# One shared ring of five PSUM buffers for scores and maxima, and the router's first batch, three gathers, tile 0's first half-product and the weight re-packing moved to other steps

## The chip, the cores and the metric

The kernel runs on 1 core of one Trainium2 chip. The metric is the device time of one execution in microseconds (us), of which the kernel before has three timed runs and one profiled execution.

## The reference

Three stages follow one another on the same 1536 tokens of 512 numbers.

```python
# 1. attention within hash buckets: 2 batches, 8 heads, 768 rows of 64
mask = q_bucket[:, :, :, None] == k_bucket[:, :, None, :]
scores = np.where(mask, q @ k.T / 8, -1e9)
attn = exp(scores - scores.max(-1)); attn /= attn.sum(-1) + 1e-9
x = attn @ v                                  # -> 1536 x 512
# 2. mixture of experts: 8 experts, each token goes to one
logits = x @ w_gate + modality_bias[modality_id]
e_idx = argmax(logits); gate = softmax(logits)[e_idx]
out[tokens of e] = gate * (relu(x @ w1[e]) @ w2[e])     # 512 -> 1024 -> 512
# 3. dense layer
h = out @ w_in                                # 512 -> 2048
out = (max(h, 0) + alpha * min(h, 0)) @ w_out
```

## The kernel before, in words

Everything is written for one core with the order of each engine's work fixed by hand: the program is emitted step by step, and each engine runs its part in that order. Wherever full precision is wanted, an fp32 operand is split in a rounded half ("hi", usually a copy on ScalarE) and a remainder ("lo", a subtraction), and a product becomes three matmuls.

**Attention** is a loop of 102 steps. Step s handles key block s % 6 (128 keys) of head s // 6 (16 heads, so scores end with step 95). In each step:
- `ST(s,0)` and `ST(s,1)` make the scores of one block against two halves of 384 queries (two matmuls each, lines 807 and 808) in a PSUM buffer "st" from the pool `pst` of 2, and ScalarE's exp reads them (line 809).
- `MAX(u,0)` and `MAX(u,1)` make, up to 11 steps ahead of the scores, the product from which the row maxima are taken (line 775) in a buffer "mxp" from the pool `psm` of 3; VectorE reduces it (line 776). From step 7 there is one unit u in a step; the last is in step 85. The order on TensorE is ST(s,0), MAX(u,0), ST(s,1), MAX(u,1).
- `EL(s-1)` splits the exponentials E: Eh by ScalarE (line 812), El by GpSimd, and from block 88 (`ELD`) by VectorE (line 813).
- `AV(s)` multiplies them by v four steps later, for two blocks in every second step (lines 821 to 823). It has one buffer, which `NORM(h)` (lines 834 to 836) frees at the end of a head. After heads 7 and 15, NORM sends the 768 finished tokens to DRAM (`x_d`, line 838).
- Small work takes turns in a pool `misc` of 2 PSUM buffers: the split of v (701 to 706), its sums (712 to 715), the signs of the hash (748 to 755), the rows of maxima (781 to 788, with a small DMA), transposes `T` of finished tokens (172, copied at 175) and the logits `L` (186 to 192).

**The hook** runs at the end of each step s and carries what is ahead of its stage. `rr.first` is the router of batch 0 as a generator of eleven pieces, one at each step of `PLAN["first"]`: softmax and one-hots (`S`), counts by matmul (`R`), the most frequent expert ("star", `star` and `star2`), ranks (`adjust`), `GATE`, and the row numbers of three tiles of 128 tokens (`pre`). It works in a `misc` buffer, on VectorE, line 203 to 275. At step 71 the buffer BIG[0] of batch 0's tokens becomes its scratch. From step 89 on, when the router is ready, three indirect DMAs `GA` on GpSimd fetch the three tiles' tokens (line 596). `W1` at the steps of `PLAN["w1"]` splits the star expert's first weights in eight pieces of 128x512: hi by GpSimd, lo by VectorE (lines 571 and 572). At step 96 tile 0's tokens are transposed and split (556 to 558).

**Experts.** After the attention, tile t of 128 tokens needs `G1(t,0)` and `G1(t,1)` (12 matmuls each, line 1007, then relu), `TH` (8 transposes, hi/lo, lines 1018 to 1021), `G2` (24 matmuls, line 1030) and `Y`. `TX(t+1)` (986 to 993) prepares the next tile's tokens. Tiles 0 to 2 are the star's; their order around `G1(0, 0)` is written out by hand, with `W2` splitting the second weights as they land (line 569 with 128x1024). Tiles 3 to 12 are the loop `for t in range(NPRE, NBASE)`; new weights are loaded and split only where the expert of a tile differs from the last one's (`changed`): first weights by `load(t + 1, which=(1,))` and `W1s`, second by `load(t, which=(2,))` and `W2`.

**Dense weights.** In six of these tiles (`PRE`) a piece of the third stage's weights comes in beside: `CL(p)` loads 1 MB through SyncE's queue, and `CV(p, 0..4)` re-packs it, once on ScalarE (line 1134) and four times on VectorE (1136 to 1142). All share the landing place x2, so that a CL waits for the CV before it. In a tile t, CL stands at the beginning, ahead of `load(t, which=(2,))`, and CV at the end. In tile 12 (`last`), `CL(LP[0])` also goes to x2.

The third stage is 16 x 3 rounds of 24 matmuls (lines 1300 and 1326).

## Time and profile before

| | |
|---|---|
| three timed runs | 720.5, 715.89, 720.5 us (median 720.5) |
| profiled execution | 719.58 us, of which the span from the first to the last instruction is 717.5 us |
| TensorE busy | 684.8 us, 95% of the span |
| mean granted clock of TensorE | 0.967 of full speed |

A time in the trace is in us from the span's start. A matmul's shown end is modelled, and starts are closer together than the shown lengths, so a busy TensorE need not be one at its peak: what it loses is in its idle time, and in stretches with a granted clock of half speed. The clock has two levels, 0.5 and 1.0 of full speed; a window's figure is a mean over both.

### The profile page before, as it was taken

How to read it: one execution, taken by the hardware profiler on the slowest of the kernel's cores; microseconds unless marked ns; L12 is line 12 of the kernel's file. 1: busy time of each engine (PE TensorE's matmuls, PEld its weight loads, DVE VectorE, ACT ScalarE, POOL GpSimd, SP SyncE). 2: the span in 40 equal slices, each digit the busy share in tenths (PEclk: the TensorE clock that was granted, in tenths of full speed). 3: DMA queues.
4: the chain of work that ended last, by engine and by line, in shares of the span. 5: the costliest groups of instructions: out<-in, count | busy, mean ns of one | idle time of the engine just before them, and what ended most of it. 6: DMA issues, size and time to landing. Idle time of an engine off the chain costs nothing. (4 is left out here: it accounts for less than half of the span.)

```text
span 717.5 us, 13119 instructions
## 1 busy us (share of the span) xinstructions
PE 684.8 (95%) x5032; PEld 564.2 (79%) x5032; DVE 443.1 (62%) x902; ACT 329.5 (46%) x555; POOL 239.3 (33%) x212
## 2 busy tenths in 40 slices
PE   6889999999998889999989999999999999999996
PEld 4668888898887778778878877788888888888884
DVE  6768788787789677516444547999644344433432
ACT  5457887887866735225334337666411111211111
POOL 8367998887975800210100011012011010010002
PEclk8569999999999999999999999999999999999999
DMA  8257854865624123226522265434001000010001
GB/s 208 62 158 176 178 150 91 178 180 127 134 98 163 47 90 131 69 69 221 206 88 89 83 226 175 132 118 147 0 23 67 0 30 1 0 59 0 1 1 58
DMA packets 31229, 72.40 MB, mean 101 GB/s; under 512 B 6924, under 2 KB 7014, under 8 KB 30902
## 3 DMA queue, kind: packets, MB, share of 16 engines
q1 hardware_dynamic: 28068, 61.78, 30.3%
q0 software_dynamic: 2960, 9.70, 4.1%
q8 instruction: 41, 0.67, 0.4%
q14 instruction: 30, 0.25, 0.1%
q10 hardware_dynamic: 130, 0.00, 0.0%
HBM read 79.15 MB, written 12.06 MB: 127 GB/s over the span
## 5 line engine op out<-in xcount | busy, mean ns | idle before, releaser
L813 POOL TENSOR_TENSOR El<-E,Eh 128x768 f16<-128x768 f32 x88 | 144.3, 1652 | 48.6 <-ACT Eh L812 17.4
L809 ACT ACTIVATE E<-st 128x384 f32<-128x384 f32 x192 | 89.4, 491 | 67.3 <-PE st L808 65.3
L776 DVE TENSOR_REDUCE mx<-mxp 128x1 f32<-128x384 f32 x189 | 96.9, 548 | 12.8 <-PE mxp L775 12.3
L569 ACT ACTIVATE gh<-gf 128x512 fp32r<-128x512 f32 x48 | 30.3, 630 | 143.9 <-PE o L1326 133.4
L812 ACT ACTIVATE Eh<-E 128x768 f16<-128x768 f32 x96 | 81.0, 845 | 0.0
L807 PE MATMUL st<-op 97*128 97x384 f32 x192 | 76.8, 400 | 3.5 <-DMA op<-mr 2.4
L775 PE MATMUL mxp<-op 76*128 76x384 f32 x189 | 68.0, 370 | 4.8 <-DVE mx L776 3.1
L572 DVE TENSOR_TENSOR gl<-gf,gh 128x512 fp32r<-128x512 f32 x48 | 33.1, 690 | 59.7 <-ACT gh L569 57.7
L1030 PE MATMUL y<-op,hh 128*128 128x512 f32 x208 | 69.6, 402 | 0.0
L1300 PE MATMUL h<-big,op 128*128 128x512 f32 x256 | 68.6, 395 | 0.0
L1343 POOL DMA_INDIRECT out_dram<-x,did x12 | 11.8, 984 | 169.1 <-DVE x L1340 89.8
L808 PE MATMUL st<-op 128*128 128x384 f32 x192 | 68.0, 354 | 0.0
L1007 PE MATMUL g<-op,xh 128*128 128x512 f32 x192 | 63.6, 403 | 1.2 <-DVEq L1087 1.0
L1326 PE MATMUL o<-op,gh 128*128 128x512 f32 x192 | 64.2, 395 | 0.0
L821 PE MATMUL av<-vh,Eh 128*128 128x65 f16 x576 | 60.0, 198 | 1.5 <-DVE big L836 1.5
L821 PEld LDWEIGHTS <-Eh 128*128 128x128 f16 x576 | 53.5, 100 | 8.9 <-issue 6.6
L822 PE MATMUL av<-vl,Eh 128*128 128x64 f16 x576 | 59.5, 196 | 0.0
L823 PE MATMUL av<-vh,El 128*128 128x65 f16 x576 | 59.2, 196 | 0.0
L1300 PEld LDWEIGHTS h<-big,op 128*128 128x128 f32 x256 | 47.9, 187 | 11.8
L822 PEld LDWEIGHTS <-Eh 128*128 128x128 f16 x576 | 54.1, 101 | 0.1
L823 PEld LDWEIGHTS <-El 128*128 128x128 f16 x576 | 54.0, 100 | 0.0
L1184 POOL DMA_INDIRECT yg<-ys,dpos x10 | 11.7, 1168 | 122.5 <-DMA ys<-ysb 67.7
(401 smaller groups left out, 1519.8 us busy)
## 6 DMA issues: line engine op xcount, KB each, us to landing
r<-in_moe_w_dram SPq DMA_DIRECT2D x42, 1024.0 KB
op<-B SPq DMA_DIRECT2D x32, 192.0 KB
op<-in_moe_w_in_dram SPq DMA_DIRECT2D x6, 1024.0 KB
op<-A SPq DMA_DIRECT2D x28, 192.0 KB
op<-A SPq DMA_DIRECT2D x13, 384.0 KB
op<-in_moe_w_out_dram SPq DMA_DIRECT2D x4, 1024.0 KB
ys<-ysb SPq DMA_DIRECT2D x13, 256.0 KB
big<-in_q_dram SPq DMA_DIRECT2D x17, 192.0 KB
```

Of the source, the lines that this page charges most:

```text
L775: mm(p[:,0:384],t[0:76,2,c*128:(c+1)*128],t[0:76,1,a*384:a*384+384],start=True,stop=True)
L776: nc.vector.tensor_reduce(out=mx[h][:,c,a:a+1],in_=p[:,0:384],axis=AX.X,op=ALU.max)
L807: mm(p[:,0:384],t[0:97,1,js],t[0:97,2,qs],start=True,stop=False)
L808: mm(p[:,0:384],t[:,0,js],t[:,3,qs],start=False,stop=True)
L809: nc.scalar.activation(E[s][0][:,qs],p[:,0:384],AF.Exp,scale=0.125)
L812: nc.scalar.activation(eh,e,AF.Copy)
L813: (nc.vector if s>=ELD else nc.gpsimd).tensor_tensor(out=el,in0=e,in1=eh,op=ALU.subtract)
L821: mm(a[:,c*65:c*65+65],eh[:,cs],VH[h//4%2][:,j,h%4,:],start=(j==0 and c==0),stop=False,skip_group_check=True)
L822: mm(a[:,c*65:c*65+64],eh[:,cs],VL[h//4%2][:,j,h%4,:],start=False,stop=False,skip_group_check=True)
L823: mm(a[:,c*65:c*65+65],el[:,cs],VH[h//4%2][:,j,h%4,:],start=False,stop=False,skip_group_check=True)
L1030: nc.tensor.matmul(yps[t], a[:, ks], b[:, kk], start=(kk == 0 and n == 0), stop=(kk == 7 and n == 2))
L1300: nc.tensor.matmul(p, terms[t][0][:, kk, cs], terms[t][1][:, kk], start=(n == 0), stop=(n == 11))
```

## The change

1. The pools `pst` (2) and `psm` (3) become one pool `ps5` of 5 buffers, which ST and MAX take in turn in their order on TensorE.
2. The router's first batch runs at steps 57 to 73, not 72 to 87. Its scratch BIG[0] is taken over at step 56; the zeros for `ys` (filled by GpSimd) lie elsewhere in it. `star2` takes a buffer of its own, with one more small copy (`k8`).
3. The three gathers are issued at steps 78, 81 and 84.
4. For n = 6 (tokens of batch 1), the transposes are at steps 88 and 89, not 89 and 90, and the logits' halves at 94 and 92, not 95 and 91.
5. W1's hi goes from GpSimd to ScalarE, and its last four pieces are at steps 96 to 99. Of blocks 91 and 94, Eh goes from ScalarE to VectorE.
6. `G1(0, 0)` runs within the attention: 6 matmuls at step 98, before the last pair of AV, and 6 and the relu at step 100, behind it.
7. CL moves behind the next tile's `TX` and `W1s`, and so behind `load(t, which=(2,))` on SyncE; the CV of a piece runs one tile later, ahead of the next CL. In tile 12, the CV of piece 6 stands behind `Y(11)` and ahead of `CL(LP[0])`.

```diff
-    ... w1=(91, 92, 93, 94, 95, 96, 98, 99), ..., first=(72, 74, 75, 76, 78, 80, 81, 82, 84, 86, 87),
+    ... w1=(91, 92, 93, 94, 96, 97, 98, 99), ga=(78, 81, 84), ..., x6=(0, 1, 6, 4), first=(57, 58, 59, 60, 62, 63, 64, 67, 71, 72, 73),
...
-    pst = pool(psA, "pst", PS[0], space=PSUM)
-    psm = pool(psA, "psm", PS[1], space=PSUM)
+    ps5 = pool(psA, "ps5", 5, space=PSUM)
...
+        if s == 56:
+            BIG[0] = big(0)
+            rr.late(rtmp, BIG[0])
+            R["z"] = BIG[0][:, 784:1296]
+            nc.gpsimd.memset(R["z"], 0.0)
+            R["first"] = rr.first(misc)
...
-        if s >= 89 and rr.ready and "pre" not in R:
-            R["pre"] = s
-            for t in range(NPRE):
-                GA(t)
+        if s in PLAN["ga"]:
+            GA(PLAN["ga"].index(s))
...
+        if s in (98, 100):
+            h, lo = R["x0"]
+            w1h, w1l = R["w1"]
+            if s == 98:
+                R["g0"] = GP()
+            p = R["g0"]
+            for kk in range(s - 98, s - 96):
+                ks = slice(kk * 128, kk * 128 + 128)
+                for n, (a, b) in enumerate(((h, w1h), (lo, w1h), (h, w1l))):
+                    nc.tensor.matmul(p, a[:, ks], b[:, kk, 0:512], start=(kk == 0 and n == 0), stop=(kk == 3 and n == 2))
+            if s == 100:
+                R["hr0"] = BIG[0][:, 1536:2048]
+                nc.scalar.activation(R["hr0"], p, AF.Relu)
...
-            W1(i // 4, i % 4, i % 4 + 1, nc.vector, nc.gpsimd)
+            W1(i // 4, i % 4, i % 4 + 1)
...
-        p=psm.tile([128,512],F32,tag="mxp",name="mxp") if pool is None else pst.tile([128,512],F32,tag="st",name="stm")
+        p=ps5.tile([128,512],F32,tag="s",name="mxp")
...
-        p=pst.tile([128,512],F32,tag="st",name="st")
+        p=ps5.tile([128,512],F32,tag="s",name="st")
...
-        nc.scalar.activation(eh,e,AF.Copy)
+        if s in (91,94): nc.vector.tensor_copy(eh,e)
+        else: nc.scalar.activation(eh,e,AF.Copy)
...
-    G1(0, 0)
+    hr[0] = R["hr0"], mp.tile([128, 1024], F32, tag="hr", name="hr", bufs=2)[:, 0:512]
...
-        if t in PRE:
-            CL(PRE[t])
         if t == last:
             G2(t - 1)
             Y(t - 1)
+            for i in range(5):
+                CV(PRE[t - 1], i)
             CL(LP[0])
         load(t, *er[t], which=(2,))
...
+        if t - 1 in PRE and t < last:
+            for i in range(5):
+                CV(PRE[t - 1], i)
+        if t in PRE and t < last:
+            CL(PRE[t])
...
-        if t in PRE:
-            for i in range(5):
-                CV(PRE[t], i)
```

## Rows read from the trace of the kernel before

**Rows 1.** The page: busy time of the engines, and the granted clock in 40 slices.

```profile
PE 684.8 (95%) x5032; PEld 564.2 (79%) x5032; DVE 443.1 (62%) x902; ACT 329.5 (46%) x555; POOL 239.3 (33%) x212
...
PEclk8569999999999999999999999999999999999999
```

**Rows 2.** Windows of steps 57-64, 65-72, 73-85, 86-101: length, PE, PEld, DVE, ACT, POOL, clock.

```profile
164.10:181.98 17.88, 17.04 (x240) 14.85 (x238) 14.08 (x41) 13.32 (x26) 13.71 (x9) 1.00 0.44 93
181.98:199.41 17.43, 17.11 (x230) 14.75 (x230) 13.48 (x32) 14.59 (x28) 15.86 (x11) 1.00 0.63 138
199.41:233.65 34.24, 31.00 (x441) 27.21 (x441) 30.24 (x109) 22.96 (x44) 22.17 (x15) 1.00 0.40 136
233.65:262.55 28.90, 24.63 (x376) 20.95 (x372) 22.68 (x42) 17.63 (x33) 15.56 (x16) 0.88 0.11 30
```

**Rows 3.** Windows of VectorE, sums: the router's first five bursts, then its last three.

```profile
sum 9.20, DVE 7.89; mean DVE 1.58
...
sum 2.97, DVE 2.56; mean DVE 0.85
```

**Rows 4.** Waits of TensorE: line waited at, releaser, us in total, times, longest.

```profile
PE mxp L775 <- DVE mx L776: 3.1, 6, 1.4
...
PE av L821 <- DVE big L836: 1.5, 1, 1.5
...
PE misc L172 <- DVE big L175: 1.3, 2, 1.0
```

**Rows 5.** Timeline of VectorE, steps 91 to 93: start, us, line, tiles.

```profile
246.19 4.47 DVE L813 TENSOR_TENSOR El<-E,Eh 128x768 f16<-128x768 f32 x1
...
251.59 0.95 DVE L813 TENSOR_TENSOR El<-E,Eh 128x768 f16<-128x768 f32 x1
```

**Rows 6.** Timeline of GpSimd, steps 90 to 93.

```profile
241.68 1.69 POOL L596 DMA_INDIRECT big<-x_d,idp  x1 [0.18 <-issue]
...
245.89 5.23 POOL L571 CAST op<-r 128x512 fp32r<-128x512 f32 x8
```

**Rows 7.** Windows of all engines: two stretches near the end of the attention.

```profile
246.00:252.00 6.00, 5.67 (x65) 4.68 (x66) 6.00 (x5) 3.31 (x6) 5.12 (x8) 0.72 0.24 72
256.00:262.00 6.00, 6.00 (x118) 5.94 (x118) 6.00 (x10) 1.33 (x2) 0.00 (x0) 0.72 0.01 3
```

**Rows 8.** The page, costliest groups: two copies on ScalarE.

```profile
L569 ACT ACTIVATE gh<-gf 128x512 fp32r<-128x512 f32 x48 | 30.3, 630 | 143.9 <-PE o L1326 133.4
L812 ACT ACTIVATE Eh<-E 128x768 f16<-128x768 f32 x96 | 81.0, 845 | 0.0
```

**Rows 9.** Timeline of TensorE: tile 0's first half, straight after the last AV.

```profile
262.55 3.02 PE L1007 MATMUL g<-op,op 128*128 128x512 f32 x12
```

**Rows 10.** Timeline of all engines, start of tile 0's second product.

```profile
277.58 1.28 DVE L1021 TENSOR_TENSOR hl<-tr,hh 128x512 fp32r<-128x512 f32 x2
...
278.98 0.48 PE L1030 MATMUL y<-op,hh 128*128 128x512 f32 x1
```

**Rows 11.** Timeline of SyncE's issues at tile 6.

```profile
344.96 0.38 SPq L1127 DMA_DIRECT2D op<-in_moe_w_out_dram  x1
345.64 1.06 SPq L585 DMA_DIRECT2D r<-in_moe_w_dram  x2
```

**Rows 12.** Timeline of all engines, tile 7 to tile 8.

```profile
363.56 1.23 DVE L1142 SCALAR_TENSOR_TENSOR op<-op 128x1024 int32<-128x1024 int32 x1
...
365.44 0.50 PE L1007 MATMUL g<-op,xl 128*128 128x512 f32 x1 [1.81 <-DVEq L1223]
```

**Rows 13.** Window behind that wait.

```profile
366.00:371.00 5.00, 5.00 (x16) 3.95 (x15) 0.82 (x2) 0.60 (x1) 0.00 (x0) 0.66 0.65 210
```

**Rows 14.** Timeline of VectorE at tile 12.

```profile
426.87 0.71 DVE L1136 TENSOR_SCALAR x<-x 128x1024 f32<-128x1024 f32 x1 [4.50 <-ACT x L1134]
```

**Rows 15.** Timeline of TensorE, step 52: second scores and second maxima.

```profile
153.37 0.34 PE L807 MATMUL st<-op 97*128 97x384 f32 x1
...
153.72 0.33 PE L775 MATMUL mxp<-op 76*128 76x384 f32 x1
```

More of the change, by code (lines that the diff above doesn't have):

```diff
@@ L523, in hook @@
             rr.xT[1] = [b2[:, i * 768:i * 768 + 768] for i in range(4)]
-            BIG[0] = big(0)
-            rr.late(rtmp, BIG[0])
-            R["z"] = BIG[0][:, 2048:2560]
-            nc.gpsimd.memset(R["z"], 0.0)
-            R["first"] = rr.first(misc)
         for n in range(7):
             bt, kc = divmod(n, 4)
-            x = PLAN["x3" if n == 3 else "x4" if n == 4 else "x"]
+            x = PLAN[{3: "x3", 4: "x4", 6: "x6"}.get(n, "x")]
             d = s - 12 * n - 16
@@ L562, in hook, with GP @@
                 R["w1"] = [slot16(i).rearrange("p (k f) -> p k f", k=4) for i in (2, 3)]
-            W1(i // 4, i % 4, i % 4 + 1, nc.vector, nc.gpsimd)
+            W1(i // 4, i % 4, i % 4 + 1)
     xg = {}
+    def GP():
+        return ps5.tile([128, 512], F32, tag="s", name="g0")
     def split(hi, lo, src, eng, first=None):
@@ L604, in misc @@
     def misc():
-        return ps1.tile([128,512],F32,tag="misc",name="misc",bufs=PS[2])
+        return ps1.tile([128,512],F32,tag="misc",name="misc",bufs=PM)
     def load(h):
@@ L770, in _program, with MAX @@
     mx={};flT={}
[L771 removed]
+    def MAX(u,a):
         h,c=divmod(u,6); t=OP[h%NP]
         if c==0 and a==0: mx[h]=wp.tile([128,6,2],F32,tag="mx",name="mx")
[L774 removed]
+        p=ps5.tile([128,512],F32,tag="s",name="mxp")
         mm(p[:,0:384],t[0:76,2,c*128:(c+1)*128],t[0:76,1,a*384:a*384+384],start=True,stop=True)
@@ L859, in _program @@
     for u in range(3):
-        for a in range(2): MAX(u,a,pst if a else None)
+        for a in range(2): MAX(u,a)
     POSTa(0,0,3); mrow(0)
@@ L998, in G1 @@
         if half == 0 and k0 == 0:
-            hr[t] = mp.tile([128, 1024], F32, tag="hr", name="hr", bufs=2)
+            h_ = mp.tile([128, 1024], F32, tag="hr", name="hr", bufs=2)
+            hr[t] = h_[:, 0:512], h_[:, 512:1024]
         hs = slice(half * 512, half * 512 + 512)
@@ L1008, in G1 @@
         if k1 == 4:
-            act.activation(hr[t][:, hs], p, AF.Relu)
+            act.activation(hr[t][half], p, AF.Relu)
     def TH(t):
@@ L1017, in TH @@
             for kk in range(4):
-                nc.tensor.transpose(p[:, kk * 128:kk * 128 + 128], hr[t][:, half * 512 + kk * 128:half * 512 + kk * 128 + 128], ident)
+                nc.tensor.transpose(p[:, kk * 128:kk * 128 + 128], hr[t][half][:, kk * 128:kk * 128 + 128], ident)
             hs = slice(half * 512, half * 512 + 512)
```

15 lines of the change are left out of this document (8 added, 7 removed).

## The prediction

> **What bounds the kernel now.** I read the page first: TensorE is busy for 684.8 of the 717.5 us span, and its clock is at half speed early on and nearly nowhere else [rows 1]. So time can come from three places only: TensorE's idle time, half-speed stretches, and idle time that the change itself makes. Then I cut the part that the change touches into windows by steps, and looked in each at which engine is fullest. In steps 57 to 72 it is TensorE, idle for 17.88 - 17.04 = 0.84 and 17.43 - 17.11 = 0.32 us, while VectorE has 3.80 and 3.95 us to spare. In steps 73 to 85 TensorE is idle for 3.24 us and VectorE is busy for 30.24 of 34.24. From step 86 to the last AV TensorE is idle for 4.27 us, at a mean clock of 0.88 [rows 2]. The list of waits says what those gaps hang on: VectorE each time, by a reduction, a NORM or a copied transpose that came late [rows 4]. Last come two gaps among the experts, read in timelines [rows 12 to 14]. From the third stage's start to the end TensorE is dense, and nothing there changes.
>
> All sums are against the profiled execution, 719.58 us (its span and 2.1 us around it). It lies 0.9 us below the median of the timed runs, 720.5; these spread over 4.6 us, so that 1% (7.2 us) is about what a measurement of this kernel can tell from no change.
>
> **The change part by part.**
>
> *Router into steps 57 to 73.* The pieces to the onehot are five bursts on VectorE with 9.20 us from first to last instruction (7.89 busy), the rest three with 2.97 [rows 3]; k8 adds one small copy, under 0.2. The five now fall in steps 57 to 64, where VectorE has 3.80 us to spare [rows 2]. 9.20 - 3.80 = 5.4 us don't fit, by busy time 7.89 - 3.80 = 4.1. VectorE can fall behind by about a step (the reduction of MAX(s,0) is wanted by the second score or maximum of step s+1), which by the mean of 17.88 / 8 = 2.2 us and what of it is lost in its own small waits I take as an estimate of 1 us; and the later steps' 3.95 us take the other 2.2 us of GATE and pre. Queued behind the bursts on VectorE are the reductions and the releases of the two misc buffers, and TensorE waits for both. So +4, with bounds +1 (all slack is used) and +6 (none, and a softmax that waits for ScalarE).
>
> *Router out of steps 73 to 85.* TensorE's idle time there is 3.24 us [rows 2], and VectorE loses about 10 of its 30 us. I take -3.2, bounds -2 (transposes and logits that stay) and -4. The gathers come here: 1.69 us for the first [rows 6], on a GpSimd with 34.24 - 22.17 = 12 us to spare [rows 2]; behind each is an El that AV wants only four steps later. No cost; without that cover some 1 us each. The memset at step 56 waits for the first `x_d` transfer, four steps after its issue; El has the same four steps, so no cost there either, and at most 2 us. The star's number is read by SyncE at step 74, long after it is known.
>
> *End of the attention.* Here one El took 4.47 us on VectorE, others 0.95, while GpSimd ran eight copies for W1 over 5.23 us [rows 5, 6]. With hi on ScalarE those copies leave GpSimd, and VectorE gets 3.5 us back. The Trainium skill, "SBUF — State Buffer", section "Who interferes with whom", says that a VectorE operation with two SBUF inputs and a GpSimd operation share a pair of ports which one of them holds for its whole length. The rows agree with it; were it otherwise and the El had waited for its Eh, nothing of the 3.5 us would come back, and the total would be that of the second rival.
> Of TensorE's 4.27 idle us I expect 2.6 back: the late copies of transposes (1.3, the steps move ahead of El 88) and most of the wait for NORM of 1.5 [rows 4]. Two stretches of 6 us ran at a mean clock of 0.72, so 2 x (1 - 0.72) x 6 = 3.4 us of each at half speed, and 1.7 us of work lost in each [rows 7]; they stand behind the blocked El and the NORM gap, and I expect half of the 3.4 back: 1.7. Tile 0's 12 matmuls took 3.02 us as shown, the modelled end of the last one included, so a little under 0.25 each [rows 9]; six of them now run ahead of the last AV pair, where TensorE would wait for El: 1.4. But the second product of tile 0 began 0.1 us after its last operand was made [rows 10], and that hangs on W2's load, which is issued after NORM(15) and doesn't move closer; I give 0.6 back. Against it, ScalarE gets 8 x 0.63 = 5.0 us and loses 2 x 0.845 = 1.7 [rows 8]; four of the eight are before the last Eh, so 2.5 - 1.7 = +0.8, and I charge 0.7. The two Eh on VectorE cost between 0.5 (three quarters of 0.71, one source [rows 14]) and 0.95 each [rows 5], nearer the first, since one source is read; the 3.5 us that came back cover them. Sum: -2.6 - 1.7 - 1.4 + 0.6 + 0.7 = -4.4, bounds -1.5 and -7 (idle time and clock all back).
>
> *One ring of five.* With one unit a step, ST(s,1) waits for the reduction that MAX(s,1) waited for, 0.35 us sooner [rows 15], and MAX waits for exps that ST waited for, later. When the maxima end, scores have five buffers, which serves the part above. All waits of a maximum for a reduction were 3.1 us in six, the longest 1.4 in step 83 [rows 4], so the first steps can gain or lose at most 3.1 - 1.4 = 1.7. I take 0.
>
> *CL and CV.* At tile 6, CL of the next piece was issued at 344.96, when the CV before it was done, and the load of tile 6's second weights stood behind it until 345.64 [rows 11]. So the split of W2 ended late, a CV came behind it until 364.8, and only then the lo of tile 8's tokens: TensorE waited for 1.81 us [rows 12], and the next 5 us had a clock of 0.66, which is 2 x 0.34 x 5 / 2 = 1.7 us of work lost [rows 13]. Now that load stands ahead of the CL, and the CV behind TX: -3.5, bounds -2.5 and -4. Behind the moved CL on SyncE are Y's store and the next tile's loads; the expert changes only here, so nothing waits for them.
> In tile 12 it goes the other way. The CV of piece 6 (VectorE: two operations of 0.7 and two of 1.23 [rows 12, 14], 3.9 us) now begins after Y(11), in VectorE's idle 4.50 us before 426.87 [rows 14], but behind a copy on ScalarE of about 1.1. So it ends some 0.5 us late, the lo of tile 12 with it: +0.5, bounds 0 and +1.2. CL(LP[0]) is issued some 4 us later, and wanted only in the third stage.
>
> Total: +4 - 3.2 - 4.4 + 0 - 3.5 + 0.5 = -6.6, and 719.58 - 6.6 = **713.0 us**.
>
> **The rivals.**
> 1. *The router is hidden and the clock comes back.* VectorE's many short waits take in the bursts (+0.5), and the end of the attention stays dense and keeps full speed (-6). For it: VectorE has 7.75 us to spare in steps 57 to 72 for 12.2. Against: 9.2 of them come in the first half. 719.58 + 0.5 - 3.2 - 6 - 3.5 + 0.5 = 707.9.
> 2. *The end of the attention is full anyway.* ScalarE has W1 on top of exp and Eh, VectorE two Eh and the Els, and gaps only change their releaser: -1.5 in place of -4.4. For it: VectorE is busy for 22.68 of 28.90 us there [rows 2] and for all of both slow stretches [rows 7]. 715.9.
> 3. *The re-packing gives nothing.* The load comes sooner, but the CV ahead of G2 delays the hl of a tile, or CL meets the load in the DMA queues: 0 in place of -3.5, so 716.5. Against: VectorE sat idle before most tiles' hl.
> 4. *The shared ring lets VectorE hold up the scores too.* Where VectorE is behind by more than a step, each ST(s,1) stands where MAX(s,1) stood, 0.35 us sooner [rows 15]. If that begins at step 57 and lasts to the end of the maxima, it costs 28 x 0.35 = 9.8, with the router at its +6: 719.58 + 6 + 9.8 - 3.2 - 4.4 - 3.5 + 0.5 = 724.8, slower. It decides as soon as the bursts outrun the spare time by more than the ring holds. Against: in steps 73 to 85 VectorE was as full, and TensorE lost 3.2 us in all.
>
> **How the numbers follow.** Forecast 0.45; rivals 1 to 4: 0.17, 0.18, 0.10, 0.10. The bounds of all parts together would give 719.58 + 1 - 4 - 7 - 1.7 - 4 = 703.9 and 719.58 + 6 - 2 - 1.5 + 1.7 - 2.5 + 1.2 = 722.5; for 8 in 10 I leave out most of rival 4 and the far ends: **706 to 719.5**. Faster by over 1% of 720.5 means below 713.3: rival 1 and rather more than half of the forecast, 0.43. Slower by over 1% is only the far part of rival 4 or an accident of the clock early on, 0.07. The rest, 0.50, lies within 1%.
>
> **What the profile after would show.** Router right: VectorE without idle time in steps 57 to 64, and those steps some 22 us long, not 17.9; steps 73 to 85 near 31 us with no wait over 0.5. End right: no GpSimd copy of W1, every El near 0.95, and from step 86 to the last AV near 25 us. Re-packing right: TensorE without a gap at tile 8 and a clock of 1.0 behind it; the load of tile 6's second weights issued near 4 us sooner against its tile. Ring right: few waits of ST for a reduction; many of them speak for rival 4. What would make me wrong: a half-speed stretch that comes or goes in the first 60 us [rows 1], a wait for misc buffers that spreads through steps 57 to 72, or a late lo of W1 that stops TensorE ahead of the last AV pair.

## The result and the profile after

The changed kernel takes 714.37 us in the median of 14 runs (712.13 to 716.52), the kernel before 720.5 in the same 14 rounds, 6.1 us more. The recorded ratio is 0.9898, with a 95% interval of 0.9877 to 0.992: about 1% faster; the two medians alone would give 0.9915. Forecast were 713.0 us, in a range of 706 to 719.5. The profiled execution took 713.37 us with a span of 711.6, against 719.58 and 717.5 before.

The page of the changed kernel, busy times and granted clock, to stand beside [rows 1]:

```profile
PE 676.3 (95%) x5032; PEld 563.1 (79%) x5032; DVE 441.4 (62%) x905; ACT 332.9 (47%) x561; POOL 234.2 (33%) x204
...
PEclk8679999999999999999999999999999999999998
```

TensorE has 8.5 us less of busy time with as many instructions (5032), so no work went. The mean clock rose from 0.967 to 0.973: what it cost fell from 0.033 x 717.5 = 23.7 to 0.027 x 711.6 = 19.2 us, which is about half of the 8.5. Most of that lies in steps 0 to 23 (a clock of 0.81 before, 0.86 after), which got only 0.67 us shorter. The rest of the 8.5 us is not the clock's; shown lengths also reach over short waits, as the part on the ring shows. The windows of the same steps as in [rows 2] (57 to 64, 65 to 72, 73 to 85, 86 to the last AV; columns as there):

```profile
160.93:179.74 18.81, 17.55 (x252) 15.05 (x250) 17.53 (x67) 13.89 (x28) 15.46 (x11) 1.00 0.45 96
179.74:200.81 21.07, 18.71 (x237) 16.44 (x236) 18.64 (x59) 15.09 (x28) 15.49 (x10) 0.92 0.51 111
200.81:231.28 30.47, 29.26 (x435) 26.83 (x431) 22.96 (x62) 22.21 (x42) 23.07 (x16) 1.00 0.45 156
231.28:257.13 25.85, 23.50 (x376) 20.89 (x372) 19.70 (x37) 20.17 (x40) 7.95 (x6) 0.93 0.09 29
```

Steps 57 to 72 grew from 35.31 to 39.88 us, with VectorE at 17.53 of 18.81 and 18.64 of 21.07; steps 73 to 85 shrank from 34.24 to 30.47, the end from 28.90 to 25.85. The second row has a clock of 0.92 where it was 1.00. ScalarE's copies of a tile's y are marks among the experts. The twelfth, from the timeline of ScalarE:

```profile
414.18 0.69 ACT L1053 ACTIVATE ysb<-y,gc 128x512 f32<-128x512 f32 x1 [5.52 <-PE y L1048]
```

The first, the eighth and the thirteenth begin at 279.77, 369.98 and 431.10 us. In the kernel before the four began at 284.85, 378.99, 422.29 and 437.06. With the starts of steps 0, 24, 57, 73 and 86 they divide the span into stretches; each number is a difference of two starts in a timeline:

| stretch | before | after | difference | forecast term |
|---|---|---|---|---|
| start to step 0 | 18.36 | 17.21 | -1.15 | ring: 0 |
| steps 0 to 23 | 72.43 | 71.76 | -0.67 | ring: 0 |
| steps 24 to 56 | 73.31 | 71.96 | -1.35 | ring: 0 |
| steps 57 to 72 | 35.31 | 39.88 | +4.57 | +4 |
| steps 73 to 85 | 34.24 | 30.47 | -3.77 | -3.2 |
| step 86 to the 1st copy of y | 51.20 | 48.49 | -2.71 | -4.4 |
| 1st to 8th copy of y | 94.14 | 90.21 | -3.93 | -3.5 |
| 8th to 12th | 43.30 | 44.20 | +0.90 | +0.5 (tile 12) |
| 12th to 13th | 14.77 | 16.92 | +2.15 | (with the row above) |
| 13th to TensorE's end | 273.61 | 273.62 | 0.01 | 0 |
| sum | | | -5.95 | -6.6 |

The sum came out nearly as forecast, but three terms did not: the ring gave something, the end gave less, and tile 12 took more. The -0.67 of steps 0 to 23 is no effect of the change: over all kernels below this stretch varies by 1.9 us without an order. The waits of TensorE (as in [rows 4]: line waited at, releaser, us in total, times, longest) say where the new losses are:

```profile
PE av L838 <- DVE big L853: 3.7, 2, 1.9
...
PE y L1048 <- DVE hl L1039: 1.4, 2, 0.9
...
PE tr L1214 <- DMA yg<-ys,dpos: 1.2, 2, 0.7
```

AV still waits for NORM, now twice; the other two rows are products that wait for a tile's hl, and transposes that wait for gathered rows. Each is looked at below.

**The ring.** I had bounded its gain by the waits of maxima that the trace shows, and taken zero. A gain is there where no wait is shown. The timeline of TensorE in the kernel before, at the end of step 24 (start, us, line, tiles):

```profile
91.75 0.33 PE L775 MATMUL mxp<-op 76*128 76x384 f32 x1
92.02 0.44 PE L807 MATMUL st<-op 97*128 97x384 f32 x1
92.30 0.34 PE L808 MATMUL st<-op 128*128 128x384 f32 x1
```

And the same place in the changed kernel:

```profile
89.97 0.34 PE L791 MATMUL mxp<-op 76*128 76x384 f32 x1
90.14 0.34 PE L823 MATMUL st<-op 97*128 97x384 f32 x1
90.32 0.34 PE L824 MATMUL st<-op 128*128 128x384 f32 x1
```

Undisturbed, one matmul starts 0.17 or 0.18 us after the last. Before, the scores started 0.27 us after the maximum (91.75 to 92.02) and the next matmul 0.28 after that, so 0.2 us were lost; yet no idle time is shown, since the modelled 0.33 us of the maximum reach over the wait. In steps 24 to 56 of the kernel before, scores stand 0.27 to 0.43 us behind a maximum seven times, in the changed kernel never over 0.23. Seven times some 0.2 is the 1.35 us, nearly: scores behind a maximum and the matmul after them give 1.2 of it. The Trainium skill, "Perfetto Trace Analysis", section "Identifying the Most-Contended Engine", says that the busy share of matmuls is not a good measure of how close TensorE is to its limit, because pipelined instructions look smaller in the trace. These rows agree that it misleads, but by lengths that look larger: 0.34 us shown where starts are 0.18 apart, and a short wait lies hidden under them.

**A NORM behind the rank piece.** VectorE and TensorE around step 65 of the changed kernel:

```profile
179.51 0.16 DVE L324 COPY misc<-e 128x6 f32<-128x6 f32 x1
...
182.20 0.17 DVE L340 CAST rm<-misc 128x6 f32<-128x6 int32 x1
182.28 0.21 DVE L851 TENSOR_SCALAR r<-av,sc 128x6 f32<-128x6 f32 x1
...
183.37 0.20 PE L838 MATMUL av<-vh,Eh 128*128 128x65 f16 x1 [1.93 <-DVE big L853]
```

The rank piece (`adjust`, 14 small operations from 179.51 to 182.37) stands ahead of the NORM of head 9 on VectorE (the expectations below call it NORM(10)), and TensorE's first AV of head 10 waits 1.93 us for it. What follows is half speed: the clock of 0.92 above.

**The end of the attention.** GpSimd and VectorE, to stand beside [rows 5, 6]:

```profile
232.92 6.48 POOL L830 TENSOR_TENSOR El<-E,Eh 128x768 f16<-128x768 f32 x4
238.54 1.69 DVE L830 TENSOR_TENSOR El<-E,Eh 128x768 f16<-128x768 f32 x1 [1.57 <-ACT Eh L829]
```

No El takes 4.47 us any more; the first on VectorE takes 1.69, while the last of GpSimd's four runs, the others 0.95 or 0.96. No wait for a copied transpose ([rows 4]) is left here. But NORM(14) is as late as the NORM that I took for gone:

```profile
246.77 0.95 DVE L830 TENSOR_TENSOR El<-E,Eh 128x768 f16<-128x768 f32 x1
...
248.02 0.67 DVE L588 TENSOR_TENSOR op<-r,op 128x512 fp32r<-128x512 f32 x1
248.62 0.20 DVE L851 TENSOR_SCALAR r<-av,sc 128x6 f32<-128x6 f32 x1
...
249.69 0.24 PE L838 MATMUL av<-vh,Eh 128*128 128x65 f16 x1 [1.76 <-DVE big L853]
```

VectorE is at work without a break, and an El, a sum's split and a lo of W1 (0.67 us) come before NORM(14); AV waits 1.76 us.

**Tiles 6 to 8.** SyncE's issues at tile 6, beside [rows 11], and TensorE at tile 8, beside [rows 12]:

```profile
336.52 1.12 SPq L601 DMA_DIRECT2D r<-in_moe_w_dram  x2
345.64 0.38 SPq L1145 DMA_DIRECT2D op<-in_moe_w_out_dram  x1
...
358.44 0.39 PE L1025 MATMUL g<-op,xl 128*128 128x512 f32 x1
```

The load of the second weights stands 9 us ahead of the CL, not behind it, and tile 8's lo (`xl`) is there when TensorE comes: no wait, and the clock is 1.00 from the first to the eighth copy of y.

**Tile 12.** GpSimd's first gather of the last tokens, SyncE's load, ScalarE and VectorE, TensorE:

```profile
417.91 1.50 POOL L1202 DMA_INDIRECT yg<-ys,dpos  x1 [64.63 <-DVE x L1156]
...
419.92 0.38 SPq L1145 DMA_DIRECT2D op<-in_moe_w_in_dram  x1
420.06 0.59 ACT L1038 ACTIVATE hh<-tr 128x512 fp32r<-128x512 f32 x1
420.73 0.69 DVE L1156 TENSOR_SCALAR x<-x 128x1024 int32<-128x1024 int32 x1
421.34 1.28 DVE L1039 TENSOR_TENSOR hl<-tr,hh 128x512 fp32r<-128x512 f32 x2
422.08 0.50 PE L1048 MATMUL y<-op,hl 128*128 128x512 f32 x1 [0.87 <-DVE hl L1039]
...
426.01 0.63 PE L1214 MATMUL tr<-ident,yg 128*128 128x128 f32 x4 [0.68 <-DMA yg<-ys,dpos]
```

The hi of tile 12 (line 1038) was done at 420.65, but VectorE was in the re-packing of piece 5 (its second operation, line 1156), which that of piece 6 had pushed back, so the lo (line 1039) began at 421.34, and TensorE waited 0.87 us. CL(LP[0]) with its 1 MB was issued at 419.92, when the first gather had been issued and its rows had not come, and transposes of gathered rows waited 0.68 us, and once more 0.51. The first gather itself took 1.50 us beside two operations of the re-packing with two inputs each (lines 1158 and 1160), where it took 0.95 before.

What the DMA engines moved from 421.5 to 424.0 us (packets, MB, share of 16 engines; q1 carries SyncE's transfers, q0 the gathers, 320 packets for all four):

```profile
q1 hardware_dynamic: 378, 0.77, 91.2%
q0 software_dynamic: 2, 0.01, 1.4%
```

The first gather's rows had come by then (80 packets), and those of the second, issued at 419.71, came behind SyncE's 1 MB.

### The profile page after: what moved, and what is told of

Its sections match the earlier page's. It is cut to its first block, busy times and chain, and to the rows that moved or that the text cites. A ratio compares the mean times of both kernels' runs of the same rounds, so it can differ in the third digit from the quotient of the medians.

```text
span 711.6 us, 13120 instructions
## 1 busy us (share of the span) xinstructions
PE 676.3 (95%) x5032; PEld 563.1 (79%) x5032; DVE 441.4 (62%) x905; ACT 332.9 (47%) x561; POOL 234.2 (33%) x204
## 5 line engine op out<-in xcount | busy, mean ns | idle before, releaser
L829 ACT ACTIVATE Eh<-E 128x768 f16<-128x768 f32 x94 | 79.5, 846 | 0.1
L823 PE MATMUL st<-op 97*128 97x384 f32 x192 | 74.8, 390 | 2.8 <-DMA op<-mr 2.5
```

Source lines behind the costliest of these rows:

```text
L823: mm(p[:,0:384],t[0:97,1,js],t[0:97,2,qs],start=True,stop=False)
L829: else: nc.scalar.activation(eh,e,AF.Copy)
```

## The experiments

Every kernel ran against the kernel before on the same chip. The latter had medians of 722.89 us beside the first four, 722.65 beside the next four and 720.45 beside the last four. So the ratio is what compares. A ratio is uncertain by 0.2 to 0.4%, 1.5 to 3 us; the stretches tell the parts apart.

| kernel | median us | ratio (95%) | start to step 0 | 24-56 | 57-72 | 73-85 | 86 to 1st y | 1st-8th y | 8th-12th | 12th-13th |
|---|---|---|---|---|---|---|---|---|---|---|
| before | | 1 | 18.36 | 73.31 | 35.31 | 34.24 | 51.20 | 94.14 | 43.30 | 14.77 |
| changed | 714.37 | 0.9898 | 17.21 | 71.96 | 39.88 | 30.47 | 48.49 | 90.21 | 44.20 | 16.92 |
| 1 two pools | 718.59 | 0.9950 (0.9926-0.9973) | 17.90 | 73.29 | 41.61 | 31.13 | 49.05 | 89.89 | 44.20 | 16.28 |
| 2 rank piece later | 713.73 | 0.9888 (0.9846-0.9930) | 17.42 | 71.88 | 39.03 | 30.41 | 48.45 | 90.14 | 44.19 | 16.09 |
| 3 late pieces as before | 712.24 | 0.9870 (0.9827-0.9913) | 16.98 | 71.94 | 40.05 | 30.44 | 48.99 | 90.12 | 43.60 | 14.77 |
| 4 W1 on GpSimd | 717.09 | 0.9933 (0.9909-0.9957) | 16.78 | 71.86 | 40.00 | 30.45 | 50.93 | 90.12 | 44.19 | 17.19 |
| 5 router as before | 712.43 | 0.9867 (0.9824-0.9909) | 17.15 | 71.89 | 34.49 | 36.61 | 49.37 | 90.01 | 44.20 | 17.25 |
| 6 router spread | 717.26 | 0.9925 (0.9898-0.9952) | 17.05 | 71.93 | 44.31 | 30.19 | 48.90 | 90.08 | 44.22 | 17.25 |
| 7 first half behind | 713.00 | 0.9855 (0.9814-0.9897) | 17.42 | 71.89 | 42.50 | 30.45 | 46.44 | 90.06 | 44.20 | 18.08 |
| 8 before, pieces late | 718.73 | 0.9940 (0.9913-0.9968) | 18.35 | 73.31 | 35.31 | 37.02 | 51.23 | 90.34 | 43.31 | 14.74 |
| 9 three mends | 708.76 | 0.9848 (0.9818-0.9878) | 17.42 | 71.90 | 39.34 | 30.40 | 46.50 | 89.98 | 43.60 | 14.77 |
| 10 two mends | 710.13 | 0.9859 (0.9826-0.9892) | 17.43 | 71.89 | 38.96 | 30.46 | 48.30 | 90.19 | 43.60 | 14.76 |
| 11 mended, old router | 708.16 | 0.9831 (0.9797-0.9864) | 16.99 | 71.94 | 34.01 | 36.60 | 46.69 | 90.01 | 43.60 | 14.77 |
| 12 mended, W1 later | 708.31 | 0.9828 (0.9799-0.9856) | 17.01 | 71.90 | 40.31 | 30.45 | 46.48 | 89.84 | 43.59 | 14.77 |

Steps 0 to 23 vary between 71.07 and 72.98 us without an order by kernel, and are left out.

### 1. The two pools back

```diff
-    ps5 = pool(psA, "ps5", 5, space=PSUM)
+    pst = pool(psA, "pst", 2, space=PSUM)
+    psm = pool(psA, "psm", 3, space=PSUM)
...
-        p=ps5.tile([128,512],F32,tag="s",name="mxp")
+        p=psm.tile([128,512],F32,tag="mxp",name="mxp") if pool is None else pst.tile([128,512],F32,tag="st",name="stm")
...
-        p=ps5.tile([128,512],F32,tag="s",name="st")
+        p=pst.tile([128,512],F32,tag="st",name="st")
...
```

The buffer of tile 0's half-product comes from `psm` here, and the first three units of maxima use both pools in turn, as in the kernel before.

> The changed kernel with the two old pools back (two buffers for scores, three for maxima). Between the first scores and step 57 the changed kernel took 143.72 us and the kernel before 145.74, though nothing but the pools differs there; step 0 also began 1.15 us sooner. Theory: the shared ring did that, as TensorE has more room when one of the two readers is late. Then step 0 to step 57 takes 145.7 us again and the time is 2 us over the changed kernel's 714.4, so 716.4. Rival 1: the two profiles differ by chance in the first steps (transfers); then step 0 to 57 stays near 143.7 and the time at 714.4. Rival 2 (the slower case of the prediction, in small): the ring lets VectorE hold up scores in steps 57 to 72; then these steps, 39.88 us in the changed kernel, get 1 to 3 us shorter with the pools.

The time is 718.59 us, and the ratio rises from 0.9898 to 0.9950: the ring is worth about 0.52%, 3.7 us, uncertain by some 2 us. Steps 24 to 56 take 73.29 us, as in both other kernels with two pools (73.31), and 71.86 to 71.96 in all eleven with the ring, so chance is out there. Step 0 begins at 17.90 to 18.36 with the pools and at 16.78 to 17.43 with the ring. Rival 2 does not appear: steps 57 to 72 take 41.61 us with the pools, not less than 39.88. What the ring gives beside the router's bursts these two profiles can't tell: with the pools the clock of steps 57 to 72 is 0.92, so 2 x 0.08 x 41.61 = 6.7 us at half speed, against 3.4 us, and run 7 below shows as large a difference with the ring in both. Without the router there, steps 57 to 72 take 34.49 and 34.01 us with the ring (runs 5 and 11) and 35.31 in both kernels with pools (before and run 8). With the pools another instruction waits for VectorE behind the bursts:

```profile
185.14 0.69 PE L792 MATMUL mxp<-op 76*128 76x384 f32 x1 [3.33 <-DVE mx L793]
```

One maximum waits 3.33 us for a reduction, as maxima have three buffers of their own here; the wait of 1.93 us for NORM is not in this trace.

### 2. The rank piece one step later

```diff
-    ... first=(57, 58, 59, 60, 62, 63, 64, 67, 71, 72, 73)
+    ... first=(57, 58, 59, 60, 62, 64, 66, 67, 71, 72, 73)
```

> The changed kernel with the router's rank piece (adjust) at step 64 in place of 63 and the onehot at 66 in place of 64. In the changed kernel NORM(10) stands behind the rank piece on VectorE; TensorE waits 1.93 us for it at 181.44, and behind that wait the window 179.74 to 200.81 has a mean clock of 0.92, so 2 x 0.08 x 21.07 = 3.4 us at half speed and 1.7 us of work lost. Theory: it is that one place; with NORM(10) ahead of the piece both come back, steps 57 to 72 take 39.88 - 3.6 = 36.3 us and the time is near 710.8. Rival 1: VectorE has too much work in these steps (36.17 of 39.88 us busy), so the wait only moves to a reduction or another NORM: steps 57 to 72 stay near 39.9, time 714.4. Rival 2: the wait goes but the half-speed stretch has another cause: 712.4.

The wait for that NORM is gone and the clock of the window from 179 to 201 us is 1.00, but steps 57 to 72 take 39.03 us, 0.85 less and not 3.6. Mostly rival 1, then: the wait and the half-speed time had lain over VectorE's own work, which goes on at its own pace. The time, 713.73 us, and the ratio, 0.9888, cannot tell this kernel from the changed one. Runs 9, 10 and 12 below have the same router steps: there steps 57 to 72 take 39.34, 38.96 and 40.31 us, the last with a clock of 0.96 in them, 2 x 0.04 x 40.31 = 3.2 us at half speed again. So the gain is under 1 us where it shows at all. Three rows of TensorE:

```profile
185.12 0.44 PE L823 MATMUL st<-op 97*128 97x384 f32 x1 [0.44 <-ACT E L825]
...
186.38 0.44 PE L791 MATMUL mxp<-op 76*128 76x384 f32 x1 [0.64 <-ACT E L825]
...
253.87 1.43 PE L568 MATMUL g<-op,op 128*128 128x512 f32 x5 [1.33 <-DVE op L558]
```

Two waits for exps take its place in step 67. The third row is from the end of the attention: TensorE, here at full speed, comes to tile 0's first half 1.33 us before tile 0's lo is made. In the changed kernel that wait was not to be seen, because half-speed time ahead of it had used it up; step 86 to the first copy of y takes 48.45 us all the same (48.49).

### 3. The late pieces as before

```diff
+        if t in PRE and t > 7:
+            CL(PRE[t])
         if t == last:
             G2(t - 1)
             Y(t - 1)
-            for i in range(5):
-                CV(PRE[t - 1], i)
             CL(LP[0])
...
-        if t - 1 in PRE and t < last:
+        if t - 1 in PRE and t < 8:
...
-        if t in PRE and t < last:
+        if t in PRE and t < 8:
             CL(PRE[t])
...
+        if t in PRE and t > 7:
+            for i in range(5):
+                CV(PRE[t], i)
```

> The changed kernel with the re-packing of the dense weights moved only in tiles 5 to 7; the pieces of tiles 8 to 11 stand as in the kernel before. From the start of tile 12's G1 to the third stage the kernel before took 14.72 us and the changed kernel 16.92; with what tile 11 lost the third stage came 2.75 us later against the tiles. Theory: that is the price of piece 6's re-packing in tile 12 and of the load that it delays into the four last gathers; undone, the third stage comes 2.7 us sooner, and the time is near 711.7, with the gain at tile 8 (3.68 us) untouched. Rival 1: the last gathers were late for another reason (a fixed time from Y(11)'s store), so 714.4. Rival 2: with the old order in tiles 8 to 11 some of the gain at tile 8 goes, and the time is 713 to 716.

The 12th to the 13th copy takes 14.77 us, as in the kernel before (14.77), the 8th to the 12th 43.60, and the gain at tile 8 stays (90.12). That is 2.75 us by the profile; the median is 712.24 us, and the ratio, 0.9870, is 2.0 us below the changed kernel's 0.9898, within what it can tell. The rows of SyncE, GpSimd and TensorE in tile 12:

```profile
415.73 0.39 SPq L1145 DMA_DIRECT2D op<-in_moe_w_in_dram  x1
418.37 0.94 POOL L1202 DMA_INDIRECT yg<-ys,dpos  x1 [64.07 <-DMA ys<-ysb]
421.90 0.50 PE L1048 MATMUL y<-op,hl 128*128 128x512 f32 x1 [0.22 <-DVE hl L1039]
```

CL(LP[0]) is issued 2.6 us ahead of the first gather, not 2 us behind it; the gather takes 0.94 us; hl is 0.22 us late, as before; no transpose waits for gathered rows, though the gathers begin later than in the changed kernel (418.37 and 417.91). Between 421.5 and 424.0 us the gathers' queue moves 149 packets here, and SyncE's none; in the changed kernel it was 2 and 378. So the rows were late behind CL(LP[0]), and not by a fixed time from the store (rival 1).

### 4. W1's hi on GpSimd again

```diff
-            W1(i // 4, i % 4, i % 4 + 1)
+            W1(i // 4, i % 4, i % 4 + 1, nc.vector, nc.gpsimd)
...
-        if s in (91,94): nc.vector.tensor_copy(eh,e)
-        else: nc.scalar.activation(eh,e,AF.Copy)
+        nc.scalar.activation(eh,e,AF.Copy)
```

> The changed kernel with the hi copies of W1 on GpSimd again and both Eh (blocks 91 and 94) on ScalarE again; the steps of W1's pieces and all else stay. Theory: GpSimd's copies hold up VectorE's El (4.47 us for one El in the kernel before, 0.95 in the changed one). Since the gathers no longer hold the copies together, they come one by one, so several El or lo take longer, 3.5 us in all; VectorE, busy for 19.70 of 25.85 us in this part, becomes late, and the time is 2 to 4 us longer: 717. Rival 1: copies that come singly fit between the El, every El stays near 0.95, and ScalarE has 5 us less to do: 713.5 to 714.4. Rival 2: TensorE in this part hangs on NORM(14) alone (1.75 us); then only that wait moves, by as much as VectorE is later.

The ratio rises by 0.35%, 2.5 us; step 86 to the first copy takes 50.93 us in place of 48.49. One El holds VectorE for 5.59 us while GpSimd runs its eight copies, and TensorE waits 2.81 us for a copied transpose behind it:

```profile
237.42 5.59 DVE L829 TENSOR_TENSOR El<-E,Eh 128x768 f16<-128x768 f32 x1 [1.56 <-ACT Eh L828]
238.24 5.23 POOL L587 CAST op<-r 128x512 fp32r<-128x512 f32 x8
...
243.53 0.83 PE L186 MATMUL misc<-wg,big 128*128 128x8 f32 x6 [2.81 <-DVE big L175]
...
L587 POOL CAST op<-r x8: 600/604/1327, 238.2 to 242.1; 128x512 fp32r<-128x512 f32 x8
```

The theory was right in the sum and wrong in the form: the copies didn't come singly, and one El bore it all. The last row is the copies' own (ns of the shortest, the median and the longest): seven took 0.60 us or little more, one after another, and the eighth, in which the El came to its end at 243.01, took 1.33. The next El takes 0.94 again. The Trainium skill, "SBUF — State Buffer", section "Who interferes with whom", says that a VectorE instruction with two SBUF inputs contends with a GpSimd instruction that reads SBUF, and that the shared ports are an exclusive lock. The rows agree: the El was held up, here over seven GpSimd copies in a row.

### 5. The router as before

```diff
-    ... first=(57, 58, 59, 60, 62, 63, 64, 67, 71, 72, 73)
+    ... first=(72, 74, 75, 76, 78, 80, 81, 82, 84, 86, 87)
...
-        if s in PLAN["ga"]:
-            GA(PLAN["ga"].index(s))
+        if s >= 89 and rr.ready and "pre" not in R:
+            R["pre"] = s
+            for t in range(NPRE):
+                GA(t)
```

> The changed kernel with the router's first batch at steps 72 to 87 again and the three gathers together from step 89 on; ring, W1 on ScalarE, tile 0's half in the attention and the re-packing stay. The move cost 4.57 us in steps 57 to 72 and gave 3.77 in steps 73 to 85, so by itself almost nothing. Theory 1: that is all; steps 57 to 72 go back to 35.3, steps 73 to 85 to about 33, and the time is 713.5 to 714.5. Theory 2: the move also paid at the end, since the gathers no longer stand in GpSimd's queue before step 93 and VectorE is not behind at step 86; then the end (25.92 us from step 86 to the last AV) is 1 to 3 us longer and the time 716. Theory 3: with the ring of five, VectorE's bursts at steps 72 to 87 are hidden as well; then the time is under 712.

712.43 us, a ratio of 0.9867 whose interval covers the changed kernel's. Steps 57 to 85 take 71.10 us against 70.35, and the end 49.37 against 48.49; the profile gives the move 1.6 us, the times take 2.2 away. Theory 2 is not borne out in size. Steps 73 to 85 have a clock of 0.91 here, as in runs 8 and 11 and not in the profile of before (1.00). The move is worth nothing that these runs can tell, and run 11 below says the same.

### 6. The router spread

```diff
-    ... ga=(78, 81, 84), ... first=(57, 58, 59, 60, 62, 63, 64, 67, 71, 72, 73)
+    ... ga=(80, 83, 86), ... first=(57, 58, 60, 62, 65, 68, 70, 72, 75, 76, 77)
```

> The changed kernel with the router's eleven pieces further apart (steps 57, 58, 60, 62, 65, 68, 70, 72, 75, 76, 77; gathers at 80, 83, 86). With the rank piece one step later the wait for NORM(10) and the half-speed stretch behind it went, but steps 57 to 72 took 39.03 us in place of 39.88, since two waits for exps came and VectorE was as full. Theory: VectorE's own time is the bound in steps 57 to 72 (36.2 of 39.9 us busy); moving 4 us of pieces into steps 73 to 79, where it has 7.5 us to spare of 30.47, gives some 2.5 us: steps 57 to 85 take 68 us in place of 70.35 and the time is near 712. Rival 1: what is moved is paid there in full: 70.3 again, 714.4. Rival 2: the four steps' grace is used up and late gathers hold up tile 0: over 715.

717.26 us and a ratio of 0.9925, 1.9 us above the changed kernel's; the intervals overlap, but steps 57 to 85 take 74.50 us in place of 70.35, where the theory said 68. Steps 57 to 72 alone take 44.31. VectorE and TensorE:

```profile
192.29 0.14 DVE L324 COPY misc<-e 128x6 f32<-128x6 f32 x1
...
194.96 0.16 DVE L340 CAST rm<-misc 128x6 f32<-128x6 int32 x1
...
198.80 0.56 DVE L722 TENSOR_TENSOR vl<-misc,vh 128x384 f16<-128x384 f32 x1
199.50 0.53 PE L764 MATMUL misc<-A,pwh 128*48 128x384 f32 x1 [3.53 <-DVE vl L722]
```

The rank piece now stands at step 68, and behind it on VectorE come reductions, a NORM, and the split of v (`vl`), which frees a misc buffer; the signs of the hash need that buffer, stand next in TensorE's order, and wait 3.53 us. Behind them the window from 194.00 to 206.30 us has a clock of 0.72. Neither rival had it: which queue a burst stands in front of matters more than how far apart the bursts are.

### 7. Tile 0's first half behind the attention

```diff
-        if s in (98, 100):
-            h, lo = R["x0"]
...
-    hr[0] = R["hr0"], mp.tile([128, 1024], F32, tag="hr", name="hr", bufs=2)[:, 0:512]
+    G1(0, 0)
```

> The changed kernel with tile 0's first half-product behind the attention again (12 matmuls after the last AV); all else stays. In the changed kernel VectorE is busy without a break from 241.2 to 256.5 us, 15.3 us, and TensorE's end there hangs on its Els. Theory of the prediction: six matmuls (1.4 us) ran in time that TensorE would have waited, less 0.6 for the second weights; undone, the start of the second product comes 0.8 us later: 715.2. Rival 1: nothing was gained, since tile 0's second product waits for hl and W2 anyway: 714.4. Rival 2: the half stands ahead of the last AV pair in TensorE's order and waits for tile 0's lo (1.33 us in the run with the rank piece later); undone, the time is 713 to 713.7.

From step 86 to the first copy of y this kernel takes 46.44 us, 2.05 less than the changed one: rival 2, with a larger price than it named. The median, 713.00 us, and the ratio, 0.9855, which is 3.1 us below the changed kernel's, agree with it, within some 3 us. The profiled execution alone took 715.44 us, because of an accident ahead: behind the same wait of 1.93 us for NORM, with the same code, half speed lasted longer, and steps 57 to 72 took 42.50 us in place of 39.88 to 40.05 (the changed kernel, runs 3 and 4). The window behind that wait:

```profile
180.40:192.00 11.60, 9.56 (x91) 8.65 (x91) 9.82 (x33) 6.87 (x12) 8.12 (x6) 0.60 0.91 199
```

2 x (1 - 0.60) x 11.6 = 9.3 us at half speed in this window, against 3.4 in the changed kernel.

### 8. The kernel before with the pieces of tiles 5 and 6 late

```diff
-        if t in PRE:
+        if t in PRE and t > 7:
             CL(PRE[t])
...
+        if t - 1 in PRE and t < 8:
+            for i in range(5):
+                CV(PRE[t - 1], i)
+        if t in PRE and t < 8:
+            CL(PRE[t])
...
-        if t in PRE:
+        if t in PRE and t > 7:
             for i in range(5):
                 CV(PRE[t], i)
```

> The kernel before with one part of the change alone: the pieces of tiles 5 and 6 are loaded and re-packed later; the pieces of tiles 8 to 11 stay. Theory: at tile 8 TensorE waited for 1.81 us behind a late split of W2 and a re-packing, and lost 1.7 more at half speed; both go, without the price in tile 12: 3.5 to 3.7 us less than before, a ratio of 0.995. Rival 1: only the wait goes: 1.8 us less, 0.9975. Rival 2: another wait comes in its place (the load of the next weights): no difference.

0.9940, 4.3 us less; the first to the eighth copy takes 90.34 us in place of 94.14, so 3.8, and nothing is paid in tile 12 (14.74). The theory holds, wait and half speed both. Steps 73 to 85 took 37.02 us here, with a clock of 0.91, and 34.24 in the profile of before, with 1.00, on the same code: that stretch of the profile of before was a lucky one by up to 2.8 us.

### 9 to 12. The mends together

Three mends (run 9) are the edits of runs 2, 3 and 7 in one kernel; two mends (run 10) are those of 2 and 3.

> The changed kernel with three mends: the pieces of tiles 8 to 11 as in the kernel before, tile 0's first half-product behind the attention, and the router's rank piece one step later. From the profiles: the pieces cost 0.9 us between the 8th and the 12th store of a tile and 1.3 to 3.3 us between the 12th and the 13th; the half-product inside costs some 2 us (from step 86 to the first store 48.49 us, 46.44 with it behind); the rank piece 0.85. Theory (the three stand in different stretches and add): 3.0 + 2.0 + 0.9 = 5.9 us less than the changed kernel, 708.5, a ratio of 0.981. Rival 1: the half-product's 2 us was chance of the clock in one profile, and comes back as a wait: 710.5. Rival 2: TensorE, earlier by all this, waits longer for the gathers, the weights or the stores: 712.

> The changed kernel with two of the three mends, the pieces and the rank piece; tile 0's first half-product stays within the attention. Against the run with three mends it tells what that half-product does. Theory: it stands ahead of the last AV pair in TensorE's order and waits there for tile 0's lo (1.33 us in the run with the rank piece later), and its six matmuls do not fill other idle time: from step 86 to the first store 48.5 us, against 46.4 with three mends, and 2 us more in all, 710.5. Rival: 46.4 came by chance, the two differ by less than 0.5 us.

Three mends take 708.76 us. The ratio of 0.9848 is 3.6 us below the changed kernel's, where 5.9 were forecast; its interval (0.9818 to 0.9878) leaves out the forecast 0.981. By the profile the pieces give 2.75 and the half-product 2.0, as in the single runs, the rank piece 0.5 (39.34 against 39.88). Three and two mends differ only in the half-product, and by 1.80 us from step 86 to the first copy (46.50 and 48.30); the times, 708.76 and 710.13, agree with that but are too uncertain to show it alone. TensorE with two mends:

```profile
254.08 1.41 PE L568 MATMUL g<-op,op 128*128 128x512 f32 x5 [1.33 <-DVE op L558]
...
259.35 0.87 PE L172 MATMUL tr<-ident,big 128*128 128x128 f32 x6 [0.69 <-ACT big L571]
```

And with three, where the twelve matmuls stand together behind the last AV:

```profile
254.83 3.04 PE L1012 MATMUL g<-op,op 128*128 128x512 f32 x12
257.72 0.88 PE L172 MATMUL tr<-ident,big 128*128 128x128 f32 x6
```

Inside, the half waits 1.33 us for tile 0's lo (line 558), ahead of the last AV pair; and behind the attention the next transposes wait 0.69 us, by the row for the relu of this half (line 571, done at 259.29). NORM(15), whose tokens they take, was done at 258.15, so it is not what they wait for; that their buffer is the one which the relu has to read first is likely, but not shown. Together 2.0, of which 1.8 is seen.

Run 11 is run 7 and 3 with the router in its old place (the edit of run 5).

> The changed kernel with the pieces of tiles 8 to 11 and the half-product as in the kernel before, and the router at steps 72 to 87 with its gathers from step 89 on, as in the kernel before: what is left of the change is the ring, W1's hi on ScalarE and the pieces of tiles 5 and 6. Theory: with the ring the router's place is worth nothing by itself, so within 1 us of the run with three mends, 708 to 709.5. Rival 1: the move was worth its place once its wait for NORM(10) is gone: 710 to 711 here. Rival 2: in its old place the ring hides it better than in steps 57 to 72: 706 to 707.

708.16 us, 0.9831: the theory, within its 1 us. Steps 57 to 85 take 70.61 us against 69.74 with three mends. What is left of the change there is the ring, W1's hi on ScalarE with two Eh on VectorE, the pieces of tiles 5 and 6, and smaller moves (the steps of n = 6 and of W1's last pieces) that no run tests alone. The first three were worth 3.7, 2.5 and 4.3 us in runs 1, 4 and 8, 10.5 together with some 2 us of uncertainty each, and this kernel is 0.0169 x 720.45 = 12.2 us faster than the kernel before.

Run 12 moves two pieces of W1:

```diff
-    ... w1=(91, 92, 93, 94, 96, 97, 98, 99)
+    ... w1=(91, 92, 94, 95, 96, 97, 98, 99)
```

> The run with three mends, and the third and fourth piece of W1 one step later (94, 95 in place of 93, 94), so that one lo of W1 (0.67 us) no longer stands ahead of NORM(14) on VectorE, for which TensorE waits 1.76 us. Theory: the wait shrinks by 0.6 us and the time by 0.6. Rival: VectorE is full there, the lo stands ahead of the Els of the last AV pair instead, and nothing is gained (within 0.3).

The rival, by the stretch: 46.48 against 46.50. Two rows of TensorE:

```profile
249.97 0.20 PE L825 MATMUL av<-vh,Eh 128*128 128x65 f16 x1 [1.16 <-DVE big L840]
...
254.47 0.20 PE L827 MATMUL av<-vh,El 128*128 128x65 f16 x1 [0.75 <-DVE El L817]
```

The wait for NORM(14) fell from 1.76 to 1.16 us, and a wait of 0.75 for an El came in the next pair. VectorE is full there. (Half speed came back in steps 57 to 72 of this profile, 40.31 us, as said at run 2.) The ratio of 0.9828 is the best of all, but its interval (0.9799 to 0.9856) covers run 9's 0.9848.

## Why the prediction was right, step by step

The time and its direction were right, and the sum of -6.6 (measured: -5.95) rests on six terms of which three held and three failed. The sum is in part luck: the ring gave 3.17 us that were not forecast (with steps 0 to 23, which vary by more), the end gave 1.69 less than forecast and tile 12 took 2.55 more.

- **Router into steps 57 to 73:** +4 forecast, +4.57 measured, within its bounds, and with VectorE nearly full as forecast (17.53 of 18.81 us). But the place was not: steps 57 to 64 were to take some 22 us and took 18.81, and steps 65 to 72 took 21.07 in place of 17.43. I had it as VectorE falling behind by a step; the one long wait is for a NORM, behind the rank piece, and removing it gave 0.85 or less (runs 2, 9, 10, 12). With the two old pools it is +6.3 (41.61, run 1); how much of the difference is the ring's and how much an accident of half speed stays open.
- **Router out of steps 73 to 85:** -3.2 forecast, -3.77 measured. The stretch of before varies by 2.8 us with the clock (run 8), so this agreement is partly luck. The move in all is worth nothing that can be measured (runs 5 and 11).
- **End of the attention:** -4.4 forecast, -2.71 measured. The El of 4.47 us did hang on GpSimd's copies (run 4). The step that failed is tile 0's half: "six of them now run ahead of the last AV pair, where TensorE would wait for El: 1.4", less 0.6. There was no such gap: without the half-product TensorE waits for two Els there, with 0.12 and 0.15 us of shown idle time (0.31 and 0.34 from start to start, where 0.03 is usual), so 0.6 us in all (run 9). With it, it waits for tile 0's lo, which VectorE makes later than the Els. It cost 1.8 to 2.05 (runs 7, 9, 10) where I had it gain 0.8. Without it the end gives 51.20 - 46.50 = 4.7 us, where the other terms were -2.6 - 1.7 + 0.7 = -3.6. "Most of the wait for NORM" didn't come back (1.5 before, 1.76 after); the clock did, in part (0.88 before, 0.93 after, 1.00 in run 9).
- **One ring of five:** 0 forecast with bounds of 1.7 either way; 3.7 us by run 1, so out of its bounds. The step that failed is its reading of waits: I bounded the gain by the maxima's shown waits for reductions and overlooked scores that start 0.1 to 0.25 us late under a modelled end. The traces show 1.35 us in steps 24 to 56 and about 1 us in steps 57 to 72 without bursts (runs 5 and 11). Rival 4's mechanism did not appear: no score of the changed kernel is shown waiting for a reduction.
- **CL and CV:** -3.5 at tile 8 forecast, -3.93 measured (-3.8 in run 8). Tile 12 was mis-sized: +0.5, bounds 0 and 1.2, against 0.90 + 2.15 = 3.05. The lo of tile 12 was late as forecast, 0.87 us against 0.23, so +0.64; what I left out is that CL(LP[0]), "wanted only in the third stage", is itself a transfer, and issued 4 us later it meets the last gathers (2 of their packets in 2.5 us, against 149 in run 3). The 2.15 us are 1.3 to 3.3 in the other kernels that share this order. Of them the listed waits explain 0.64 + 0.68 + 0.51 = 1.8. The 0.90 between the 8th and the 12th copy I didn't forecast at all; 0.6 of it goes with the old order (run 3), the remaining 0.3 stays open.

Of the rivals, 1 is out in both halves: the router cost 4.57 us and not 0.5, and the end gave 2.71 and not 6. Rival 2 is half true, the end lying between its 1.5 and my 4.4. Rival 3 is out at tile 8, but both of its mechanisms came in tile 12: a late hl, and CL meeting other transfers. The start, 1.15 us sooner, goes with the ring in all its eleven kernels; that the first six units of maxima find five buffers there, and not three beside two, is likely the reason, but nothing tests it by itself.

What stays open: why half speed behind the same 1.93 us wait lasts 3.4 us in one execution and at least 9.3 in another, and whether the router's move is worth 1 us either way.

## What to carry to other kernels

Pooling buffers that two readers free at different times can pay even where the trace shows no wait: compare the distance from start to start with the smallest one, not the shown idle time. A burst put on an almost full engine is paid for by whatever stands behind it in that queue, so check each instruction that frees a buffer for another engine (NORM, a split, a copied transpose) before choosing the step. Where a transfer is delayed to make room, look at what else uses the queues at its new time; a matmul moved forward into a supposed gap needs its latest operand to be there, not only the engine to be idle.

## What was unexpected of the hardware

- A wait of about 0.1 us before a score cost about 0.2: all seven scores that started late behind a maximum in steps 24 to 56 of the kernel before were followed by a matmul 0.28 us later and not 0.18 (91.75, 92.02, 92.30 above), with no idle time shown.
- One two-input operation on VectorE (El, 0.95 us alone) took 5.59 us beside a row of eight GpSimd copies; it was let in behind the seventh, and the eighth took 1.33 us in place of 0.60 (run 4).
- An indirect gather's issue on GpSimd took 1.50 us beside two-input operations of VectorE's re-packing, and 0.94 or 0.95 without them (runs 3 and before).
- The rows of an indirect gather all but stopped while SyncE's queue moved a load: 2 packets in 2.5 us against 149 without it (the changed kernel and run 3).
